# Moving one tile's layer-norm statistics to ScalarE, with fewer warm-up matmuls and re-picked scheduler limits, in a transformer block

## The chip, the cores and the metric

One core of one Trainium2 chip. The metric is the time of one execution on the device in microseconds (us), smallest is best. Executions of one kernel differ, so medians of several are compared, and ratios with a 95% interval.

## The reference

A transformer block with adaptive layer norm, batch 1, 2048 tokens of 512, 32 heads of 16, a gated FFN of 1792:

```python
mod = (silu(c) @ w_mod).reshape(1, 6, 1, 512)        # sa, ca, ga, sb, cb, gb
h = layernorm(x) * (1 + ca) + sa
x = x + ga * (attention(h, wqkv) @ wo)               # softmax over 2048 keys, 32 heads
h = layernorm(x) * (1 + cb) + sb
x = x + gb * ((gelu(h @ w_gate) * (h @ w_up)) @ w_down)
```

## The kernel before

The kernel is a program that writes a program. A recorder takes each instruction, works out its waits and keeps a clock for each engine (`self.free`), by which the scheduler decides what comes next.

Softmax needs 2048 tiles of 128x512 exponentials. ScalarE (ACT) does most, two or three to an instruction, straight from PSUM. VectorE takes some in fours (a quad) by a bit trick: it converts scores to the bits of a bf16 power and adds shifts, which VectorE or GpSimd makes. While this runs, TensorE does the projections, the output projection and the FFN as side work. The parts that matter here, with cuts marked `...`:

```python
FILL, FLOOR = 4200, 3300          # filler matmuls are added where TensorE has too little work
CREDIT = 2048
SLIP = 0
PLAN = ((8, 6, 18), (9, 5, 16), (5, 5, 22), ... (7, 5, 24))   # three limits for each sixteenth of the run

def prologue(self):
    ...
    self.warm_up(14)                                      # 56 column-tiled matmuls of 512 columns
    self.act(self.tcol[:, :], self.scp[:, 0, 0:NDC], ACT.Tanh, scale=0.5)
    for t in range(2):
        self.ln_stat(t)                                   # VectorE: bn_stats, bn_aggr
    self.ln_rstd(0, 2)                                    # GpSimd: add eps, pow
    ...
    for t in range(2, 4):
        self.ln_stat(t)
    self.ln_rstd(2, 4)
    self.mod_cols(self.scp[:, 1, 0:8], 0)                 # 32 one-column matmuls, need w_mod
    for t in range(4):
        self.ln_norm(t, self.tb1[:, 0, t, :])
    self.copy(dve, self.modA[:, :], self.scp[:, 1, 0:8])
    ...
    self.warm_up(3)
    for dc in range(NDC):
        for t in range(4):
            self.transpose(...)                           # then modulate, K and Q projection, scores
...
def stream(self):
    while cg <= group[units[-1]]:
        self.limit = PLAN[min(len(PLAN) - 1, pos * len(PLAN) // nseq)]
        ...
        elif (cand and self.quad_free and (pos < ends[LATEK] or self.credit < CREDIT or idle) and ...):
            rnd = rounds[cand.pop(0)]                     # VectorE takes a quad
        ...
        if g is not None:                                 # before VectorE converts a score tile:
            while (self.free["dve"] + 1260 <= self.free["act"] + SLIP
                   and self.step("dve", max(self.free["dve"], t) + 40)):
                pass                                      # room for another VectorE task first?
```

At the end `tail` does what is left of the last two sets of 128 tokens: denominators, output projection, second layer norm, FFN.

The softmax here doesn't subtract the row's maximum and nothing guards it: scores larger than these inputs give would overflow.

## Time and profile before

| | before |
|---|---|
| median (3 runs) | 801.11 us (800.34 to 801.63) |
| execution that was profiled | 802.81 us, span 801.0 us |
| first exponential on ACT | 14.0 us |
| last exponential ends | 773.7 us |
| ACT busy between the two | 754.0 of 759.7 us |
| from there to the end | 27.3 us |

The traced execution was the slowest of four, 1.7 us above the median.

### The profile page before, as it was taken

The page shows a single profiled execution, that of the slowest core. Times are in us where ns is not written, and L with a number is a line of the kernel's source. Part 1 is how long each engine was busy: PE and PEld are TensorE (multiplying, and loading weights), DVE is VectorE, ACT ScalarE, POOL GpSimd, SP SyncE. Part 2 cuts the span into 40 slices and gives each one's busy share as a digit, 9 for nine tenths or more (in the row PEclk, how much of TensorE's full clock was granted, in tenths as well). Part 3 has the DMA queues.
Part 4 walks back from the last instruction along what each step waited for, and adds up shares of the span by engine and source line. Part 5 has one row for each costly group of instructions (what it writes and reads, how often), then busy time and mean ns, then how long its engine had stood idle before and what let it go on. Part 6 is the DMA issues. An engine that isn't in the chain of part 4 may idle for free.

```text
span 801.0 us, 27439 instructions
## 1 busy us (share of the span) xinstructions
PE 746.0 (93%) x12243; PEld 268.8 (34%) x12247; DVE 690.8 (86%) x1254; ACT 765.8 (96%) x729; POOL 272.5 (34%) x169
## 2 busy tenths in 40 slices
PE   8899999989999999999998989999998999999987
PEld 3333333322222222222222222222344333345555
DVE  6878999988899889889898998998899997779753
ACT  4999999999999999999999999999999999999972
POOL 3100243375484542715555203544562002000100
PEclk9999999999999999999999999999999999999999
DMA  9100000000012111120022112110132221120000
GB/s 312 59 9 11 17 9 17 11 16 10 16 54 70 47 29 49 49 55 21 19 67 68 50 35 55 46 45 16 36 96 64 71 63 37 32 80 14 11 20 14
DMA packets 58632, 36.03 MB, mean 45 GB/s; under 512 B 17977, under 2 KB 55090, under 8 KB 58514
## 3 DMA queue, kind: packets, MB, share of 16 engines
q1 hardware_dynamic: 56914, 32.84, 14.8%
q8 instruction: 96, 1.57, 0.8%
q10 hardware_dynamic: 1600, 1.44, 0.6%
q14 instruction: 22, 0.18, 0.1%
HBM read 29.62 MB, written 2.61 MB: 40 GB/s over the span
## 4 chain that ended last, share of the span: by engine, by line
ACT 78%; PE 10%; DVE 7%; DMA 2%; POOL 1%; issue 1%; SPq 1%; POOLq 0%; DVEq 0%
ACT E L379 75%; PE ps_sc L366 4%; PE ps_mi L366 3%; ACT wreg L379 3%; PE ps_pv L366 2%; DVE mreg L391 2%; DVE dreg L391 1%; DMA den<-scr_den 1%; POOL mreg L391 1%; SPq L430 1%; DVE wreg L396 0%; DMA rb<-scr_rec 0%; DVE wreg L383 0%; DVE xs L383 0%; DMA scr_rec<-rden 0%
## 5 line engine op out<-in xcount | busy, mean ns | idle before, releaser
L379 ACT ACTIVATE E<-ps_sc 128x1024 bf16<-128x1024 f32 (+2 forms) x687 | 740.9, 1258 | 18.3 <-PE ps_sc L366 18.1
L391 POOL TENSOR_SCALAR mreg<-dreg 128x2048 uint16<-128x2048 uint16 x98 | 184.4, 1897 | 315.5 <-DVE mreg L391 84.0
L391 DVE TENSOR_SCALAR dreg<-ps_sc 128x512 uint16<-128x512 f32 x267 | 181.5, 686 | 38.8 <-PE ps_sc L366 36.7
L366 PE MATMUL ps_sc<-qT,kme 32*128 32x512 bf16 (+2 forms) x1319 | 174.0, 332 | 14.0 <-ACT E L379 11.2
L366 PE MATMUL ps_sc<-qT,kmo 32*128 32x512 bf16 (+2 forms) x1320 | 176.2, 331 | 8.8 <-ACT E L379 7.8
L366 PE MATMUL ps_pv<-E,vaug 128*17 128x512 bf16 (+2 forms) x2080 | 149.4, 328 | 0.9 <-DVE osb L400 0.9
L366 PE MATMUL ps_pv<-mreg,vaug 128*17 128x512 bf16 (+2 forms) x1816 | 128.1, 335 | 1.8 <-DVE mreg L391 0.7
L391 POOL TENSOR_SCALAR mreg<-mreg 128x2048 uint16<-128x2048 uint16 x38 | 71.8, 1898 | 94.8 <-DVE mreg L391 62.1
L391 DVE TENSOR_SCALAR mreg<-ps_sc 128x512 uint16<-128x512 f32 x137 | 92.5, 684 | 11.2 <-PE ps_sc L366 10.6
L366 PE MATMUL ps_mi<-wreg,mreg 128*32 128x512 bf16 (+1 forms) x1280 | 92.8, 375 | 5.5 <-DVE wreg L396 2.6
L366 PEld LDWEIGHTS ps_sc<-qT,kme 32*128 32x128 bf16 x1319 | 46.4, 91 | 141.6 <-ACT E L379 115.9
L366 PEld LDWEIGHTS ps_sc<-qT,kmo 32*128 32x128 bf16 x1320 | 46.4, 91 | 124.9 <-ACT E L379 104.1
L391 DVE TENSOR_SCALAR mreg<-dreg 128x2048 uint16<-128x2048 uint16 x121 | 80.8, 688 | 0.4
L366 PEld LDWEIGHTS ps_pv<-E,vaug 128*17 128x17 bf16 x2080 | 43.7, 89 | 56.5 <-issue 44.2
L366 PEld LDWEIGHTS ps_pv<-mreg,vaug 128*17 128x17 bf16 x1816 | 41.1, 89 | 37.2 <-issue 13.9
L391 DVE TENSOR_SCALAR mreg<-mreg 128x2048 uint16<-128x2048 uint16 x73 | 48.8, 690 | 0.6 <-PE ps_pv L366 0.5
L366 PEld LDWEIGHTS ps_mi<-wreg,mreg 128*32 128x32 bf16 x1280 | 27.1, 95 | 43.9 <-issue 20.0
L366 PE MATMUL ps_mi<-hreg,wreg 128*32 128x512 bf16 x480 | 40.5, 385 | 1.2 <-DVE vaug L400 1.1
L396 DVE SCALAR_TENSOR_TENSOR wreg<-wreg,ps_mi 128x512 bf16<-128x512 bf16 x49 | 33.4, 681 | 6.4 <-PE ps_mi L366 3.6
L400 DVE CAST wreg<-ps_mi 128x512 bf16<-128x512 f32 x49 | 33.6, 686 | 3.0 <-PE ps_mi L366 2.4
L383 DVE TENSOR_TENSOR wreg<-wreg 128x1024 bf16<-128x1024 bf16 (+1 forms) x56 | 34.0, 615 | 0.2
L379 ACT ACTIVATE wreg<-wreg 128x1024 bf16<-128x1024 bf16 (+1 forms) x28 | 29.5, 1053 | 0.0
(149 smaller groups left out, 635.2 us busy)
## 6 DMA issues: line engine op xcount, KB each, us to landing
mreg<-in_B_w_up_dram SPq DMA_DIRECT2D x22, 256.0 KB, 2.9
mreg<-in_B_w_gate_dram SPq DMA_DIRECT2D x15, 256.0 KB, 3.1
rb<-scr_rec SPq DMA_DIRECT2D x96, 32.0 KB, 1.8
dreg<-in_B_w_down_dram SPq DMA_DIRECT2D x9, 256.0 KB, 3.8
mreg<-in_w_mod_dram SPq DMA_DIRECT2D x1, 2048.0 KB, 13.4
mreg<-in_B_w_down_dram SPq DMA_DIRECT2D x8, 256.0 KB, 2.7
out_dram<-xs SPq DMA_DIRECT2D x16, 128.0 KB, 1.7
osb<-osb SPq DMA_DIRECT2D x48, 32.0 KB, 2.0
```

Of the source, the lines that this page charges most:

```text
L366: return self.rec("pe", lambda e: e.matmul(out, lhsT, rhs, start=start, stop=stop, tile_position=tp), [lhsT, rhs], [out], cost=(n, int(rhs ...
L379: return self.rec("act", lambda e: e.activation(out, in_, func, scale=scale, **kw), rd, wr, cost=self.cost("act", out, [in_], "act"))
L383: return self.rec(eng, lambda e: e.tensor_tensor(out, a, b, op), [a, b], [out], cost=self.cost(eng, out, [a, b], "tt"))
L391: return self.rec(eng, lambda e: e.tensor_scalar(out, a, s1, s2, **kw), rd, [out], cost=self.cost(eng, out, [a], "ts"))
L396: return self.rec("dve", lambda e: e.scalar_tensor_tensor(out, a, s, b, op0=op0, op1=op1), rd, [out], cost=self.cost("dve", out, [a, b], " ...
L400: return self.rec(eng, lambda e: e.tensor_copy(out, in_), [in_], [out], cost=self.cost(eng, out, [in_], "ts"))
L430: return e.dma_start(out, in_)
```

## The change

ACT sums tile 3 and its squares in the prologue, VectorE derives mean and variance with three small operations instead of bn_stats and bn_aggr, two of three warm-ups before the transposes go, and the table of limits gets two more columns (side credit for `CREDIT`, slack for `SLIP`) and new values. The intent is an earlier start and fewer waits.

```diff
-CREDIT = 2048
-SLIP = 0
-PLAN = ((8, 6, 18), (9, 5, 16), (5, 5, 22), ... twelve more, ten of them (5, 5, 22) ..., (7, 5, 24))
+PLAN = ((5, 5, 18, 1600, 0), (6, 5, 22, 2048, -300), (8, 4, 18, 2600, 0), (5, 5, 18, 1600, 0), ...
+        (8, 5, 16, 1600, -150), (5, 5, 18, 1600, 0), (5, 5, 18, 1600, 0))      # entries 2, 3 and 14 differ from the rest
         self.act(self.tcol[:, :], self.scp[:, 0, 0:NDC], ACT.Tanh, scale=0.5)
+        self.act(self.E[:, 0, :], self.xs[:, 3, :], ACT.Copy, accum=self.rden[:, 0, 0:1])
+        self.act(self.E[:, 0, :], self.xs[:, 3, :], ACT.Square, accum=self.rden[:, 0, 1:2])
...
-        for t in range(2, 4):
-            self.ln_stat(t)
+        self.ln_stat(2)
+        m, q, v = self.rden[:, 0, 0:1], self.rden[:, 0, 1:2], self.mv[:, 3, 1:2]
+        self.ts(dve, self.mv[:, 3, 0:1], m, 1.0 / D, None, ALU.mult)
+        self.stt(v, m, 1.0 / D, self.mv[:, 3, 0:1], ALU.mult, ALU.mult)
+        self.stt(v, q, 1.0 / D, v, ALU.mult, ALU.subtract)
...
-        self.warm_up(3)
+        self.warm_up(1)
...   CREDIT becomes self.limit[3], SLIP becomes self.limit[4]
```

More of the change, by code (lines that the diff above doesn't have):

```diff
@@ L63 @@
 LATE = 0
-SLIP = 0
-PLAN = ((8, 6, 18), (9, 5, 16), (5, 5, 22), (5, 5, 22), (5, 5, 22), (5, 5, 22), (5, 5, 22), (5, 5, 22), (5, 5, 22), (9, 4, 18), (7, 6, 24), (5, 5, 22), (5, 5, 22), (5, 5, 22), (5, 5, 22), (7, 5, 24))
+PLAN = ((5, 5, 18, 1600, 0), (6, 5, 22, 2048, -300), (8, 4, 18, 2600, 0), (5, 5, 18, 1600, 0), (5, 5, 18, 1600, 0), (5, 5, 18, 1600, 0), (5, 5, 18, 1600, 0), (5, 5, 18, 1600, 0), (5, 5, 18, 1600, 0), (5, 5, 18, 1600, 0), (5, 5, 18, 1600, 0), (5, 5, 18, 1600, 0), (5, 5, 18, 1600, 0), (8, 5, 16, 1600, -150), (5, 5, 18, 1600, 0), (5, 5, 18, 1600, 0))
 QA = 5
@@ L1348, in stream @@
                         g = quad["rnd"][2]
-                    elif (cand and self.quad_free and (pos < ends[LATEK] or self.credit < CREDIT or idle) and rounds[cand[0]][2] < pos + 96 and self.backlog() < BACK
+                    elif (cand and self.quad_free and (pos < ends[LATEK] or self.credit < self.limit[3] or idle) and rounds[cand[0]][2] < pos + 96 and self.backlog() < BACK
                           and all(k in self.have for k in self.keys(seq[rounds[cand[0]][2]]))):
@@ L1386, in stream @@
                     kq = self.kq[quad["k"]]
-                    while (self.free["dve"] + 1260 <= self.free["act"] + SLIP
+                    while (self.free["dve"] + 1260 <= self.free["act"] + self.limit[4]
                            and self.step("dve", max(self.free["dve"], t) + 40)):
```

## The prediction

> **What bounds the kernel now.** I read the page first (busy shares), then the ACT groups with shapes kept apart, then ACT's busy time in six stretches, then who ACT waited for, and last the timeline at the two ends.
>
> ```profile
> PE 746.0 (93%) x12243; PEld 268.8 (34%) x12247; DVE 690.8 (86%) x1254; ACT 765.8 (96%) x729; POOL 272.5 (34%) x169
> ...
> L379 ACT ACTIVATE E<-ps_sc 128x1024 bf16<-128x1024 f32 x432 | 424.6, 1111 | 1.5 <-PE ps_sc L366 1.5
> L379 ACT ACTIVATE E<-ps_sc 128x1536 bf16<-128x1536 f32 x248 | 360.8, 1533 | 4.8 <-PE ps_sc L366 4.6
> ...
> 14.00:100.00 86.00, 84.46 (x81) 1.00 0.15 49
> 100.00:250.00 150.00, 149.40 (x145) 1.00 0.09 24
> 250.00:420.00 170.00, 170.00 (x165) 1.00 0.16 42
> 420.00:600.00 180.00, 179.61 (x171) 1.00 0.18 49
> 600.00:720.00 120.00, 118.73 (x104) 0.99 0.21 59
> 720.00:773.70 53.70, 51.82 (x49) 1.00 0.06 15
> ```
>
> ScalarE (ACT) is busy 96% of the span, and 785.4 us of that are the two groups of softmax exponentials. The stretches (second column length, third ACT busy) run from the first exponential, at 14.0 us, to the last, at 773.7: 759.7 us long, 754.0 busy, so ACT stands still for only 5.7 us between its first and last exponential. The kernel is three pieces: a prologue of 14.0 us before the first exponential, a stream bound by ACT work, and a tail of 27.3 us after the last. In the stream the idle time is a handful of single waits:
>
> ```profile
> 29.21 3.29 ACT L379 ACTIVATE E<-ps_sc 128x1536 bf16<-128x1536 f32 x3 [1.53 <-PE ps_sc L366]
> ...
> 674.29 45.45 ACT L379 ACTIVATE E<-ps_sc 128x1024 bf16<-128x1024 f32 x38 [1.24 <-PE ps_sc L366]
> ...
> 769.51 4.13 ACT L379 ACTIVATE E<-ps_sc 128x1536 bf16<-128x1536 f32 x3 [1.48 <-PE ps_sc L366]
> ...
> 672.00:674.00 2.00, 2.00 (x24) 0.50 0.09 23
> ```
>
> The bracket is ACT's idle time before the group. At 29.21 the scores wait for the second K block (VectorE makes it at 27.65 to 29.1). At 674.29 the last line, TensorE's own stretch, shows its granted clock at 0.50: sixteen matmuls ahead of the scores took 1.71 us where other such sixteens took 0.8. At 769.51 the scores stood in TensorE's order behind an output projection that waited for a denominator's round trip through DRAM (the chain runs SP queue, denominator load, reciprocal store, broadcast load, onorm at 766.32). The other waits are 0.2 to 0.4 us each.
>
> [...] the trace's busy time over count is 983 ns for 1024 and 1455 ns for 1536, [...] the built program agrees that the two new activations, Copy and Square, need no load: it has two table loads, as before. [...]
>
> **The change part by part.** I compared the order of the instructions that both programs are built to; that gives counts and order, and all durations are from the trace before.
>
> *Prologue.* ACT now takes the sum and the sum of squares of tile 3, while VectorE drops one bn_stats (0.66 us) and one bn_aggr (0.18), 0.84 in sum, and gains three one-column operations of about 0.17 (such small ones took 0.15 to 0.20), 0.5 in sum. The two activations cost some 0.6 each (the 128x512 one from PSUM took 0.60) and lie in ACT's idle stretch of 5.65 us before its first modulate, so they should finish near 6.3, just as bn_aggr of tile 2 ends at 6.41. The statistics are then ready at about 6.95 rather than 7.20, and the norms of tiles 2 and 3 end near 8.9 rather than 9.2. That alone is not what releases the transposes: TensorE does three warm-ups of 512 columns after the modulation columns.
>
> ```profile
> 9.05 0.83 PE L366 MATMUL ps_mi<-dreg 128*32 128x512 bf16 x12
> 9.81 1.07 PE L370 MATMUL ps_sc<-ident,dreg 128*128 128x128 bf16 x16
> ```
>
> With one warm-up left (four instructions of the twelve), two thirds of the time from 9.05 to 9.7 go: 0.43 us. The columns start at 8.16 and end at 9.05 in either program. So the transposes start near 9.35, which needs both edits (norms at 8.9 and fewer warm-ups), and everything up to the first exponential follows in a chain: 14.0 becomes 13.6. The first seventy VectorE groups and ninety TensorE groups after that stand in the same order, so the whole start shifts, with its 1.53 us wait. **Prologue: -0.4.**
>
> *Stream, work.* The built program has 419 exponentials of 1024 where there were 432, and 258 of 1536 where there were 248. That is four more tiles of 512 on ACT, one quad fewer approximated on VectorE (436 tiles for 440). ACT's cost: 10 x 1.455 - 13 x 0.983 = 14.55 - 12.78 = **+1.8 us**. The 28 tanh of the gelu stay. GpSimd takes 152 shifts of 128x2048 for 136 (16 x 1.90 = 30 us, of over 500 idle), and VectorE 175 for 194 (19 x 0.69 = 13 us less). Neither is the bound, so this is worth time only through fewer waits of ACT.
>
> *Stream, waits.* Of 5.7 us I expect 1.5 to stay (K block). The 1.48 before the last exponentials should mostly vanish: between the last 256-wide accumulation and the projection that waited, the old order has scores for 39 tiles, the new one for 51, so the DRAM round trip is covered by 12 x 0.43 = 5 us more. The clock dip (1.24) I put at one half, with 12 more warm filler quads in the new program (272 instructions for 224). The rest, 1.4, I leave about as it is. That makes 3.5 us of idle for 5.7: **-2.2**.
>
> *Tail.* The old order still has 32 grouped down-projection matmuls and one full one to do after the last scores, and their closing pair on VectorE stands between two denominators:
>
> ```profile
> 774.61 0.96 DVE L403 RECIPROCAL rb<-ps_sc 128x128 f32<-128x128 f32 x1
> ...
> 775.49 0.63 DVE L383 TENSOR_TENSOR wreg<-ps_mi,gb 128x512 bf16<-128x512 f32 x1
> ...
> 776.15 0.42 DVE L383 TENSOR_TENSOR xs<-xs,wreg 128x512 bf16<-128x512 bf16 x1
> ...
> 776.69 0.95 DVE L403 RECIPROCAL rb<-ps_sc 128x128 f32<-128x128 f32 x1
> ```
>
> In the new order that FFN group is finished before the end of the scores and the two reciprocals are neighbours, so the last projection starts about 1.05 us earlier (0.63 + 0.42). From 782 on, TensorE's matmuls fill the tail to 796.4 in both programs, so what is saved is its 0.7 us of standing still before the transposes at 781.32 and one matmul of 0.2. **Tail: -0.8.**
>
> Sum: -0.4 + 1.8 - 2.2 - 0.8 = -1.6, from 801.1 to **799.5 us**.
>
> **The rivals.** (1) *New waits take the place of the old ones.* Each of the limits was chosen offline with a model of the engines, and the old set had been chosen so too. For it: TensorE is 93% busy and VectorE 86%, so a reordering meets other collisions[...]. Against it: the old trace shows at most 0.4 us for an ordinary wait, and VectorE gets less to do. It would keep the 5.7 us of idle or add some: 801 to 803. (2) *ACT's work alone decides,* the waits vanish better than I think and the tail shrinks: idle falls to the 1.5 of the start. That makes 797.5. (3) *The prologue gains nothing,* if ACT's statistics come late (an accumulating activation may cost more than a plain one; this trace has none) and the norms become what releases the transposes: +0.4 on my number, 799.9. In no reading is there 16 us to win: all stream idle time, the prologue's and the tail's gains together are under 8 us. For a 2% loss, ACT would have to stand still for 16 us more, three times what it does.
>
> **Range and chances.** The parts I trust least are the stream's waits (-4 to +2 against mine) and the tail (0 to -1.2). Runs before spread by 1.3 us. So 799.5, with 797.0 to 802.2 for 8 in 10. Faster by over 2%: 0.01; within 2%: 0.98; slower: 0.01.
>
> **What would show each step right or wrong.** First exponential at 13.6 (13.4 to 13.8), transposes at 9.35 and directly behind the one warm-up; Copy and Square ending before 6.9. ACT's busy time between first and last exponential 755.8 (754.0 + 1.8). ACT idle in it near 3.5, with no wait over 0.5 at the last projection, the 1.5 at the second K block kept. From the end of the last exponential to the end of the span 26.5 rather than 27.3, with the two reciprocals adjacent. What would make it wrong: a granted clock at half speed in a new place in the stream, a new wait of ACT of over 2 us, or a tail in which the order of the output stores holds up the last denominators.

The sum: -0.4 + 1.8 - 2.2 - 0.8 = -1.6 us, all estimated from the trace before and the two built programs. Putting the clock dip at one half (0.6 of the 2.2) was my estimate, and that filler matmuls spare a dip is shown by no run. The trace showed only one half-clock stretch in the stream, 0.50 at 672 to 674 us, behind a 5 us stretch in which TensorE was busy for 3.85.

## The result, and the profile after

The changed kernel was timed against the one before in three comparisons. A ratio is the mean time of one kernel's runs over that of the other's of the same rounds, so it is not quite the ratio of the medians beside it.

| comparison | before, median | changed, median | ratio | 95% interval |
|---|---|---|---|---|
| first | 801.27 us | 801.18 us | 1.0002 | 0.9985 to 1.0020 |
| second | 801.86 | 800.39 | 0.9982 | 0.9971 to 0.9994 |
| third | 801.56 | 801.10 | 0.9992 | 0.9977 to 1.0008 |

The time is the same within 2%. The plain mean of the three ratios is 0.9992, some 0.6 us, of which only the second comparison is clear of zero. The predicted 799.5 was a gain of 1.6.

The first trace of the changed kernel has a span of 798.5 us, 2.5 under that of the kernel before. That pair misleads: its execution took 800.28 us and was the fastest of four, whereas the trace before came from an 802.81 us execution. What may be compared between single traces is each step, not the span.

First the groups of ACT with shapes kept apart, in the changed kernel (`xcount | busy us, mean ns | idle before`; the file is two lines shorter, so L379 became L377):

```profile
L377 ACT ACTIVATE E<-ps_sc 128x1024 bf16<-128x1024 f32 x419 | 413.5, 1121 | 0.6 <-PE ps_sc L364 0.4
L377 ACT ACTIVATE E<-ps_sc 128x1536 bf16<-128x1536 f32 x258 | 375.5, 1553 | 2.9 <-PE ps_sc L364 2.4 <-PE ps_mi L364 0.3
```

The busy times of the two groups sum to 789.0 us for 785.4, and the idle time before them fell. Both sums are larger than ACT's whole busy time (765.8 us before, 768.6 after): neighbours overlap, and an overlap between a short and a long exponential is counted in both groups. So what ACT's work costs is read from ACT's own busy time. Second, the stretches from first to last exponential and from there to the end, all engines (length, then busy PE, PEld, DVE, ACT, POOL):

```profile
13.20:771.50 758.30, 711.60 (x11837) 246.17 (x11836) 662.23 (x1181) 755.38 (x705) 296.25 (x169) 1.00 0.16 42
771.50:798.50 27.00, 21.42 (x233) 16.32 (x237) 11.92 (x24) 8.36 (x16) 0.80 (x2) 0.97 0.03 11
```

ACT is busy 755.4 of 758.3 us, so 2.9 idle for 5.7. Third, ACT's order of time: all its waits in that stretch that are over 0.2 us.

```profile
28.42 217.88 ACT L377 ACTIVATE E<-ps_sc 128x1536 bf16<-128x1536 f32 x207 [1.53 <-PE ps_sc L364]
246.59 21.00 ACT L377 ACTIVATE E<-ps_sc 128x1536 bf16<-128x1536 f32 x20 [0.29 <-PE ps_sc L364]
584.56 9.62 ACT L377 ACTIVATE E<-ps_sc 128x1536 bf16<-128x1536 f32 x8 [0.34 <-PE ps_mi L364]
594.56 29.64 ACT L377 ACTIVATE E<-ps_sc 128x1024 bf16<-128x1024 f32 x26 [0.39 <-PE ps_sc L364]
```

The 0.58 us before the first exponential is left out. The 1.53 us at the second K block is there again to the hundredth; the waits at the clock dip and at the last projection are gone. Fourth, the prologue in order of time:

```profile
4.71 0.62 ACT L377 ACTIVATE E<-xs 128x512 bf16<-128x512 bf16 x1
5.24 0.19 ACT L377 ACTIVATION_READ_ACCUMULATOR E<-xs 128x1 f32 x1
5.46 0.63 ACT L377 ACTIVATE E<-xs 128x512 bf16<-128x512 bf16 x1
5.99 0.19 ACT L377 ACTIVATION_READ_ACCUMULATOR E<-xs 128x1 f32 x1
...
8.69 0.40 PE L364 MATMUL ps_mi<-dreg 128*32 128x512 bf16 x4
...
9.02 1.07 PE L368 MATMUL ps_sc<-ident,dreg 128*128 128x128 bf16 x16
```

From the start of the last warm-ups to the transposes it is 0.33 us (8.69 to 9.02); before it was 0.76 (9.05 to 9.81). Each accumulating activation brings an accumulator read of 0.19 us that I had not counted, and with it took 0.75 us from start to start (4.71 to 5.46); that costs nothing, as ACT then idles for 3.5 us. No table load came with Copy and Square: either trace has two, of 1.28 us each. The first exponential came at 13.2, not 13.6, because the modulation columns started at 7.81 us for 8.16, which no edit touches (see below).

Fifth, the tail in order of time:

```profile
772.40 1.77 DVE L401 RECIPROCAL rb<-ps_sc 128x128 f32<-128x128 f32 x2
...
773.41 0.23 PE L364 MATMUL ps_sc<-wreg,qT 128*128 128x128 bf16 x1 [0.55 <-ACT wreg L377]
...
778.25 0.40 PE L368 MATMUL ps_sc<-ident,E 128*128 128x128 bf16 x4 [0.50 <-DVE E L389]
...
779.42 0.38 PE L364 MATMUL ps_pv<-xs,hreg 128*128 128x512 bf16 x1
```

The reciprocals are neighbours, as predicted, but the tail is only 0.4 us shorter. Why is worked out further down.

### The profile page after: what moved, and what is told of

Read it like the earlier page. It is cut to its first block, busy times and chain, and to the rows that moved or that the text cites. A ratio compares the mean times of both kernels' runs of the same rounds, so it can differ in the third digit from the quotient of the medians.

```text
span 798.5 us, 27441 instructions
## 1 busy us (share of the span) xinstructions
PE 744.2 (93%) x12246; PEld 267.6 (34%) x12250; DVE 682.8 (86%) x1232; ACT 768.6 (96%) x730; POOL 302.5 (38%) x185
## 4 chain that ended last, share of the span: by engine, by line
ACT 87%; PE 8%; DVE 3%; DMA 1%; SPq 1%; issue 0%; DVEq 0%
ACT E L377 84%; PE ps_sc L364 4%; ACT wreg L377 3%; PE ps_mi L364 3%; PE ps_pv L364 2%; DVE mreg L389 1%; DMA den<-scr_den 1%; SPq L428 1%; DVE osb L398 0%; DVE xs L381 0%; DVE wreg L381 0%; PE ps_sc L368 0%; DVE onorm L381 0%; DVE kmo L398 0%; DVE dreg L389 0%
## 5 line engine op out<-in xcount | busy, mean ns | idle before, releaser
L377 ACT ACTIVATE E<-ps_sc 128x1024 bf16<-128x1024 f32 (+2 forms) x684 | 742.8, 1278 | 15.8 <-PE ps_sc L364 15.2
L389 POOL TENSOR_SCALAR mreg<-dreg 128x2048 uint16<-128x2048 uint16 x100 | 187.9, 1898 | 196.4 <-DVE mreg L389 79.8
L364 PE MATMUL ps_sc<-qT,kme 32*128 32x512 bf16 (+2 forms) x1316 | 170.8, 331 | 14.9 <-ACT E L377 12.1
L364 PE MATMUL ps_sc<-qT,kmo 32*128 32x512 bf16 (+2 forms) x1318 | 172.8, 331 | 9.4 <-ACT E L377 8.2
L389 POOL TENSOR_SCALAR mreg<-mreg 128x2048 uint16<-128x2048 uint16 x52 | 98.0, 1898 | 176.3 <-DVE mreg L389 46.3
L364 PE MATMUL ps_pv<-mreg,vaug 128*17 128x512 bf16 (+2 forms) x1780 | 124.3, 337 | 2.5 <-DVE mreg L389 1.5
L389 DVE TENSOR_SCALAR mreg<-ps_sc 128x512 uint16<-128x512 f32 x127 | 86.0, 686 | 17.0 <-PE ps_sc L364 16.4
L389 DVE TENSOR_SCALAR mreg<-dreg 128x2048 uint16<-128x2048 uint16 x116 | 77.4, 694 | 1.2 <-PE ps_pv L364 1.1
L364 PEld LDWEIGHTS ps_pv<-mreg,vaug 128*17 128x17 bf16 x1780 | 40.2, 89 | 39.5 <-issue 13.8
L389 DVE TENSOR_SCALAR mreg<-mreg 128x2048 uint16<-128x2048 uint16 x59 | 41.0, 709 | 1.5 <-PE ps_pv L364 1.5
L636 POOL TENSOR_SCALAR mv<-mv 128x4 f32<-128x4 f32 (+2 forms) x11 | 3.2, 291 | 92.3 <-DVE mv L421 91.0
```

The source lines that it names most:

```text
L364: return self.rec("pe", lambda e: e.matmul(out, lhsT, rhs, start=start, stop=stop, tile_position=tp), [lhsT, rhs], [out], cost=(n, int(rhs ...
L377: return self.rec("act", lambda e: e.activation(out, in_, func, scale=scale, **kw), rd, wr, cost=self.cost("act", out, [in_], "act"))
L389: return self.rec(eng, lambda e: e.tensor_scalar(out, a, s1, s2, **kw), rd, [out], cost=self.cost(eng, out, [a], "ts"))
L636: self.rec("pool", lambda e: e.tensor_scalar(v, v, EPS, None, op0=ALU.add), [v], [v], cost=200)
```

## The experiments

All timed runs are of five rounds. "Traced" numbers are of one execution each.

**1. The kernel before, against itself.** No edit. It tells what the rounds can tell apart, and whether the waits stay in place.

> The kernel before, unchanged, timed against itself: 1.000, and the width of the interval is what these rounds can tell apart. Clock theory (each run loses 0 to 2.5 us to half-clock stretches of TensorE that fall in different places from run to run): this trace has its half-clock stretch elsewhere than the 671 to 675 us of the first trace or none, and its span lies between 798.5 and 800. Rival (the waits belong to the schedule): the 1.24 us wait near 674 us and the half clock there are seen again, and the 1.48 us wait at the last projection too.

Measured: 0.9991 (0.9979 to 1.0004). So a ratio of 0.999 is nothing here. The half-clock stretch of TensorE lay at 424 to 432 us (first trace: 670 to 676) and cost ACT two waits of 1.03 us; the span was 800.3, a little over what I expected. The wait at the last projection was there again with 1.15 us. Both sides of the expectation came out in part: the clock's waits move, the projection's belongs to the schedule.

**2. New limits, old prologue.**

```diff
-        self.ln_stat(2)  # and the ACT statistics, and warm_up(1)
+        for t in range(2, 4):
+            self.ln_stat(t)    # as before, and warm_up(3)
```

> The new limits with the old prologue (the stream is instruction for instruction that of the changed kernel). My sum: -1.2 us against before (stream +1.8 of work, -2.2 of waits, tail -0.8), ratio 0.9985. Rival that the waits only change places: 0.0 to +1.0 us, ratio 1.000 to 1.001. In its trace ACT's busy time from first to last exponential is 755.4 to 755.8 us for 754.0, and idle there about 3 us.

Measured: 1.0001 (0.9986 to 1.0016), ACT busy 755.9 us, idle 4.8 for the expected 3. The forecast ratio of 0.9985 lies just outside the interval, so these rounds do not support a gain of 1.2 us from the limits alone; zero fits. Its trace shows two waits, 1.02 us at 81.8 and 0.88 at 308.3, that the first trace of the changed kernel, with the same stream, has not. The chain of waits ahead of the second:

```profile
301.41 3.42 DMA den<-scr_den
...
304.86 0.25 DVE rden L401
...
306.64 1.04 PE ps_mi L364 x6
307.68 0.59 PE ps_sc L364 x3
```

VectorE stands in its own order behind a reciprocal whose denominators come from DRAM; TensorE runs out of work, its clock falls to 0.52 at 308 to 310 us, and the six slow matmuls hold the scores. (In the first two traces of the changed kernel TensorE stood still at the same place, for 0.92 and 0.87 us where it was 1.08 here, and the clock stayed at 1.00: experiment 8.) The wait at 81.8 has the same chain (a denominator load of 3.48 us in it) with the clock at 1.00.

**3. New prologue, old limits.**

```diff
+        self.act(... ACT.Copy ...); self.act(... ACT.Square ...)   # the whole new prologue
-        self.warm_up(3)
+        self.warm_up(1)
```

> The new prologue (ACT statistics and one warm-up) with the old limits; nearly the old order in the stream. My sum: -0.4 us, ratio 0.9995, first exponential at 13.6 us, or 13.2 where the clock is full earlier in the first warm-up as in the trace of the changed kernel. Rival that the gain is taken back at the second K block or in the tail: 0.0, with ACT's wait near 29 us longer by 0.4.

Measured: **1.0063** (1.0050 to 1.0076), 807.02 us. Neither side had that. The head gained what it should (0.33 us from the last warm-ups to the transposes; the first exponential came at 13.05 us, also because the columns started early, at 7.63) and the stream was not worse (758.7 us long, 4.6 idle), but the tail took 32.3 us for 27.3. The order of the instructions says how: the clock of the scheduler was a little earlier, and in its last two per cent it chose other side work. The output projection of the last but one set now came after the last scores, so the layer norms of both last sets came together and no chunk of the FFN could be done for one of them ahead of the other. In time:

```profile
775.50 0.69 DVE L419 BATCH_NORM_STATS2 st<-ps_sc 128x6 f32<-128x512 f32 x1
776.23 0.18 DVE L423 BATCH_NORM_AGGREGATE mv<-st 128x2 f32<-128x6 f32 x1
776.33 0.66 DVE L419 BATCH_NORM_STATS2 st<-xs 128x6 f32<-128x512 bf16 x1
...
778.29 0.40 PE L370 MATMUL ps_sc<-ident,E 128*128 128x128 bf16 x4 [2.83 <-DVE E L391]
778.32 0.60 ACT L379 ACTIVATE xs<-ps_sc 128x512 bf16<-128x512 f32 x1 [5.04 <-DVE E L391]
...
780.02 2.36 PE L366 MATMUL ps_sc<-wreg,qT 128*128 128x256 bf16 x8
```

Two layer norms stand end to end on VectorE with TensorE idle for 2.83 us, and then the first eight matmuls take 2.36 us, where eight of that shape took 1.04 in the tail before: the clock has dropped (0.50 at 780 to 782 us).

**4. The same prologue with stream and tail held to the old order.** The two dropped warm-ups are still recorded, so that the scheduler's clock sees them, and only not emitted. The built program differs from the one before in the prologue alone.

```diff
-        self.warm_up(3)
+        self.warm_up(3, 2)            # two of them ghosts: recorded for the clock, left out of the program
```

> The new prologue, with the stream and the tail held to those of before, instruction for instruction: the two dropped warm-ups are still counted by the scheduler's clock and only not emitted. If the 5 us of the run with the new prologue and the old limits came from the order of the tail, which the scheduler re-chose, and not from the prologue: -0.4 us, ratio 0.9995 (0.998 to 1.0005), tail after the last exponential 27.4 us and modulation columns to transposes 1.22 us for 1.65. Rival that the new prologue itself slows what follows (a colder TensorE, later DMAs): +2 to +5 us, ratio 1.003 to 1.006, with the old tail order.

Measured: 0.9997 (0.9982 to 1.0012), tail 27.4 us. So the 5 us of experiment 3 came with the re-chosen order, not from the prologue; the +0.3 to +0.6% of the rival is excluded. The expected -0.4 fits, and so does zero.

**5. The two halves of the prologue, one look each**, with the old stream. No time is taken from them, only steps.

> One look, for its trace: one warm-up for three between modulation columns and transposes, VectorE still doing the statistics of tile 3, stream and tail those of before. If the warm-ups alone held the transposes: 1.22 us from the first modulation column to the first transpose, as with the whole new prologue, where the columns start late (after 8.1 us); where they start at 7.7 the norms, which end near 9.2 to 9.4, hold them and it is 1.3 to 1.6. First exponential 13.5 to 14.1.

> One look, for its trace: ScalarE takes the statistics of tile 3, three warm-ups kept, stream and tail those of before. If TensorE's warm-ups alone held the transposes, the 1.65 us from the first modulation column to the first transpose stays and the first exponential comes no earlier for it (13.5 to 14.5 with the columns' start), while the norms end 0.3 us earlier after the first bn_stats (5.2 us after its start for 5.6). Rival that the statistics were what held it: 1.3 us.

Fewer warm-ups alone (last warm-ups, then transposes):

```profile
9.36 0.40 PE L366 MATMUL ps_mi<-dreg 128*32 128x512 bf16 x4
9.69 1.07 PE L370 MATMUL ps_sc<-ident,dreg 128*128 128x128 bf16 x16
```

ACT's statistics alone:

```profile
9.07 0.83 PE L366 MATMUL ps_mi<-dreg 128*32 128x512 bf16 x12
9.84 1.07 PE L370 MATMUL ps_sc<-ident,dreg 128*128 128x128 bf16 x16
```

0.33 us with the fewer warm-ups, 0.77 with the statistics: in these two traces the warm-ups make the whole step. The norms ended 5.6 us after the first bn_stats started in the one (3.56 to 9.15) and 5.2 in the other (3.67 to 8.89), so the statistics do save their 0.4 us on VectorE, but TensorE is not waiting for them. In the statistics look the modulation columns were held halfway by their weights' transfer, so I read the step from the last warm-ups and not from the first column. Could the statistics count where the columns start early? The transposes go through the four tiles in turn, so tile 3 comes fourth, some 0.18 us after the first. In the first two traces of the changed kernel the columns started at 7.81 and 7.78 us, the norms ended at 9.05 and the transpose of tile 3 started at 9.20 and 9.18. With the old statistics, 0.35 to 0.4 us later, that norm would have ended near 9.4 and held this transpose for some 0.2 us. That is an estimate from these times; no run has an early start with one warm-up and the old statistics.

**6. One slack value back to 0, in the second sixteenth.** Before choosing this I built the changed kernel with all credits put back to 2048: the program came out the same, instruction for instruction. So of the two new columns only the slack does anything, at two entries.

```diff
-        (6, 5, 22, 2048, -300),
+        (6, 5, 22, 2048, 0),
```

> The changed kernel with the slack of the second sixteenth put back from -300 to 0. The program then has 411 exponentials of 1024 and 267 of 1536 for 419 and 258: 11 more tiles on ACT, 9 x 1.455 - 8 x 0.985 = +5.2 us of ACT work. Theory that the stream is ACT's work and its few waits: 5.2 us slower than the changed kernel, so about +3.7 against before, ratio 1.0046. Rival that more work on ACT is made up by fewer waits, of which only 2.9 us are there to win: at least 2.3 us slower than the changed kernel, ratio 1.001 or more; a ratio below that would kill the ACT account.

Measured: 1.0072 (1.0057 to 1.0087), 807.47 us, against the changed kernel of the same rounds (801.10) some 6.3 us slower by the means. ACT alone, from first to last exponential and to the end (length, busy):

```profile
14.03:776.86 762.83, 760.32 (x708) 1.00 0.15 42
776.86:805.40 28.54, 8.36 (x16) 0.97 0.03 10
```

760.3 us of ACT work for 755.3 in the trace of the changed kernel of these rounds: +5.0 for the expected +5.2. Idle fell by 0.9 (2.5 for 3.4), so work was not made up by waits, and the tail grew by 1.6. The closeness of 5.0 to 5.2 is partly luck: the trace has one exponential of a single tile (776.23 us) that the count left out, so 12 tiles went back and not 11, and the costs of 1.455 and 0.985 were too high (see the account below). The account of the stream holds; I had not foreseen the tail.

**7. The other slack value back to 0, in the fourteenth sixteenth.**

```diff
-        (8, 5, 16, 1600, -150),
+        (8, 5, 16, 1600, 0),
```

> The changed kernel with the slack of the fourteenth sixteenth put back from -150 to 0. One tile less on ACT (-0.5 us), but the tail is of another order: the last but one output projection comes after the last scores and only one chunk of the FFN, not two, is done for one set alone. Theory that the tail's order is what this entry buys: stream -0.5 and tail longer than 27.0 us by 1 to 5 (it was 32.3 in the run with the new prologue and the old limits), so 0.5 to 4.5 us slower than the changed kernel, ratio against before 0.999 to 1.004. Rival that the tail is TensorE-bound whatever its order: tail 27.0 and 0.5 us faster than the changed kernel, ratio 0.9975.

Measured: 1.0043 (1.0029 to 1.0057), 805.12 us, 4.0 us slower than the changed kernel of the same rounds. Stream 758.4 us (changed: 758.7), tail 31.0 (26.9). The "one tile less on ACT" was a miscount: the trace has one exponential of a single tile, at 771.94 us, so ACT has as many tiles as in the changed kernel, and its busy time was 755.6 for 755.3.

```profile
772.56:803.60 31.04, 8.39 (x16) 0.97 0.04 14
```

The whole loss is the tail, at the upper end of what the theory of the order said and against the rival that TensorE fills it whatever the order.

**8. The changed kernel again, twice** (the second and third comparisons above), as partner on each chip.

> The changed kernel, unchanged. My sum: -1.6 us, ratio 0.998, the sum of the two halves. Rival that only the traced run was a lucky one: 1.000, as the first comparison had it (1.0002), and this trace's span is 799 to 800 rather than 798.5, with a half-clock stretch and the ACT wait that it makes in a place where the first trace had none.

> The changed kernel once more, as the partner of the other three on this chip. The first comparison gave 1.0002, the second 0.9982; my sum says 0.998, no gain says 1.000. With ACT idle 2.5 to 3.0 us between first and last exponential and the tail 27.0 us, as in its two earlier traces, unless a half-clock stretch falls into it.

Measured: 0.9982 with ACT idle 2.5 us and no half clock in the stream, and 0.9992 with idle 3.4 and a half-clock stretch. The "lucky trace" rival was wrong about the second, whose span was 797.8. The third trace shows what the luck is (stretch, length, PE busy, PEld, DVE, ACT, POOL, granted clock):

```profile
302.00:304.00 2.00, 0.81 (x11) 0.19 (x7) 1.58 (x4) 2.00 (x3) 0.00 (x0) 1.00 0.00 0
304.00:306.00 2.00, 1.63 (x19) 0.46 (x23) 1.91 (x5) 1.48 (x3) 0.00 (x0) 0.81 0.09 21
306.00:308.00 2.00, 2.00 (x19) 0.23 (x11) 1.37 (x2) 2.00 (x3) 1.94 (x2) 0.50 0.14 49
```

TensorE is busy for 0.81 of 2 us, at the place where experiment 2 showed the denominator's round trip, and then the clock halves. ACT waited 0.52 and 0.46 us around it. The first trace of the changed kernel is nearly as lean at this place and keeps its clock:

```profile
302.00:304.00 2.00, 0.88 (x11) 0.20 (x8) 1.80 (x6) 2.00 (x3) 0.00 (x0) 1.00 0.05 4
```

So the lean place belongs to the order of the instructions, and whether the clock dips there differs from run to run.

All traces whose stream is exactly the old or the new one, in one table (us):

| trace | stream | first exponential | ACT busy | ACT idle | tail | half clock in the stream |
|---|---|---|---|---|---|---|
| before | old | 14.0 | 754.0 | 5.7 | 27.3 | 670 to 676 |
| before, again | old | 13.5 | 754.0 | 5.4 | 27.4 | 424 to 432 |
| prologue, frozen | old | 13.8 | 754.1 | 6.0 | 27.4 | 424 to 428 |
| warm-ups, frozen | old | 13.9 | 753.9 | 4.6 | 27.4 | none |
| statistics only | old | 14.0 | 753.6 | 5.2 | 27.5 | 764 to 770 |
| changed, first | new | 13.2 | 755.4 | 2.9 | 27.0 | none |
| changed, again | new | 13.2 | 755.2 | 2.5 | 27.0 | none |
| changed, third | new | 13.8 | 755.3 | 3.4 | 26.9 | 304 to 310 |
| limits only | new | 14.3 | 755.9 | 4.8 | 26.9 | 306 to 310 |

Means of the new stream less those of the old: busy +1.5, idle -2.0, tail -0.4. With the 0.43 of the warm-ups that is -1.3 us. The three comparisons say -0.6 on average, each with an interval of about 1.2 us to either side, so the two do not contradict each other, and the size stays open to about that. One pair has the same stream and differs in the prologue alone: the changed kernel against the limits only, in the same rounds, was 1.5 us faster by the means. The runs of these two kernels spread over 1.9 and 3.6 us, so the 0.4 us of the prologue cannot be told from that either.

## Why the prediction was right or wrong

**The total** was right within its range, and so was "the same within 2%": 801.18 us lies in 797.0 to 802.2. That range also holds the time before, 801.1, so lying in it does not show that anything was gained. The gain of 1.6 us was too large: 1.3 by the steps, about 0.6 by the clock.

**Prologue, -0.4: the size was right, the reason half wrong.** The step shrank by 0.43 us, as the term said. But "which needs both edits" failed: fewer warm-ups alone gave the same 0.33 us to the transposes, and the statistics alone left 0.77. The prediction's own times said so: the old norms ended near 9.2 us, before the 9.35 at which the transposes were to start. Where the columns start that late, ACT's statistics, the part that names the change, save 0.3 to 0.4 us on an engine that nobody is waiting for. Only in the two traces with an early start may they have been worth some 0.2 us, which no run shows. The check "first exponential at 13.6 (13.4 to 13.8)" was a bad one: the same new prologue gave 13.05 to 14.1 in different traces. The 56 matmuls of the earlier warm-up took 3.2 to 4.2 us, longer the later the granted clock first became full in the trace (4.2 to 6.7 us after its start, in the same order in all twelve traces; 3.34 us with 4.9 in the changed kernel's first, 3.69 with 5.6 in the one before), and in several traces the modulation columns then waited for their weights' transfer. Neither is in the edit.

**Stream, work, +1.8: right in kind, the cost a little too high.** It was 1.5 us over four traces. The costs of 0.983 and 1.455 us, busy time over count, were misread, as was "785.4 us of that": a group's busy time includes overlaps that the other group has too. From start to start, in the trace before, an exponential with no idle time behind it took 904 ns (1024 elements) and 1331 (1536), medians of 425 and 244 pairs. That gives 10 x 1.331 - 13 x 0.904 = 1.6 us.

**Stream, waits, -2.2: right in kind, about right in size.** The wait at the last projection, 1.15 to 2.68 us in the five old traces, is in none of the four new ones. That fits the larger distance which the prediction counted between the last wide accumulation and that projection; the distance was not varied by itself. The wait at the second K block stayed at 1.53. The clock dip, put at one half, was in two of four new traces and in four of five old ones, too few to say that it became rarer. It came back at the same places of the same order (from 424 us in two old traces, from 304 and 306 in two new ones). What decides it the traces do not settle: it followed 2 us in which TensorE was busy for 0.85 (668 to 670 us, before) or 0.81 (302 to 304, changed, third), and after 2 us with 0.76 (266 to 268, changed, first) the clock stayed at 1.00. Where a dip came, ACT's waits at it were 0.9 to 2.1 us in sum (in "statistics only" it fell into the wait at the last projection and made that the 2.68), so the dips are one part of what spreads the runs.

**Tail, -0.8: the mis-sized term.** It measured -0.44. The statistics of the last projection did start earlier after the last exponential (3.88 us for 4.80), and so did the transposes (6.74 for 7.66): 0.9 each, near the 1.05 of the two VectorE operations. But the down-projection matmuls that start the full stretch came 7.91 us after it for 8.33. I had taken TensorE's idle time before the transposes as all to be won, and it only fell from 0.72 to 0.50. The new order does less matmul work ahead of them and more behind (thirteen small FFN matmuls for four). And the leftover work that the change removed from the tail had stood where TensorE now waits for the first modulated columns, 0.55 us at 773.41; the trace before has no such wait there.

**The rivals.** New waits in place of the old ones was nearest as to the time, though GpSimd's 16 more shifts hardly slowed VectorE's own, which took 694 and 709 ns for 688 and 690. Its twelve 128x512 multiplications `onorm` went from 684 to 783 ns, 1.2 us in all on an engine that is not the bound; whether GpSimd did that was not tested. ACT's work alone (797.5) asked for 1.5 us of idle, and 2.5 to 4.8 stayed. ACT's statistics did not come late: they ended at 6.2 us. What I did not see at all is that the new limits also keep the new prologue from doing harm. The new prologue with the old limits is 5 us slower (experiment 3), since the scheduler's order for the tail flips; one slack of the fourteenth sixteenth is worth 4.0 us for the same reason and that of the second sixteenth 6.3. A change that moves the time by 0.1% stands next to orders that cost 4 to 6 us more.

**Open:** whether the gain is 0.3 or 1.3 us; and why the scheduler's order flips at just these values, which is a matter of its own clock and not of the chip.

## What to carry to other kernels

Where a program is ordered by a model of the engines, an edit of half a microsecond at its start can re-order its end; hold the order fixed (record the old instruction, leave it out of the program) to learn what the edit itself is worth, and look at the order of the tail before believing a time (the tail took 27.0, 31.0 and 32.3 us in three orders here). Do not take the busy time of a group over its count for the cost of one more instruction where shapes alternate; measure from start to start (here 0.983 and 1.455 us against 0.904 and 1.331). Before moving work off an engine, find who waits for that work: 0.4 us were saved on VectorE while TensorE's warm-ups were what stood in the way. And where runs differ by more than the effect, compare steps between several traces, never the spans of one pair.
